# Bucketed attention and MoE on one core: exponentials interleaved in pairs of key tiles, one subtraction moved to POOL, the order made anew

## The chip, the cores and the metric

The kernel runs on one core of a Trainium2 chip. The metric is the time of one execution on the device, in microseconds (us). The program drives five engines that run side by side, each through its own queue in order: PE (TensorE, matrix products; PEld is its loading of weights), DVE (VectorE), ACT (ScalarE), POOL (GpSimd), and SP (SyncE), which here only issues transfers. Results of PE land in PSUM, eight banks of 512 fp32 columns on 128 partitions; everything else works in SBUF.

## What is computed

Two stages. Attention in which a query sees only the keys of its own bucket (six sign bits of a projection), and a feed-forward layer with squared ReLU over the result:

```python
q_bits = (np.einsum('bhsd,dk->bhsk', q, proj) > 0)          # k_bits likewise
q_bucket = np.sum(q_bits * powers, axis=-1)                 # k_bucket likewise
mask = q_bucket[:, :, :, None] == k_bucket[:, :, None, :]
scores = scale * np.matmul(q, k.transpose(0, 1, 3, 2))
scores = np.where(mask, scores, -1000000000.0)
scores = scores - np.max(scores, axis=-1, keepdims=True)
attn = np.exp(scores)
attn = attn / (np.sum(attn, axis=-1, keepdims=True) + 1e-09)
x = np.matmul(attn, v)            # then (B, H, S, D) -> (B*S, H*D)
r = np.maximum(x @ w_in, 0.0)
out = (s * (r * r) + b) @ w_out
```

There are 4 batches, 8 heads, 768 positions and 64 channels; the layer has 3072 rows, 512 inputs and 2048 hidden units. All data is fp32.

## The kernel before, in words

**Tiling.** Scores are held transposed, keys on partitions and queries along the free axis. A slot is one head and one chunk of 256 queries against all 768 keys, that is six key tiles of 128, two to a PSUM bank, so three banks of 512 columns. There are 96 slots: batch 0 first does chunk 0 of its eight heads (slots 0 to 7), then chunks 1 and 2 of each head (slots 8 to 23); batches 1 to 3 do three chunks head by head (slots 24 to 95). A visit is a run of slots with the same head.

**Two halves of a number.** [...] Where precision is needed, a number is written as a high part (fp32r) and a low part (the rest), and products run over both.

**A slot.** PE makes the scores with the mask in them (`lead`, L522). DVE takes the maximum over the six tiles for each partition and query (L527, `mx`). PE transposes that (L531), DVE takes the maximum across (L533, `nmt`), PE transposes it back (L535), DVE lays it out as rows (L541), and PE subtracts it by adding a product to the scores (`rest`, L552). ACT then takes the exponential, one bank at a time, into the three pieces of tile `et` (L557). In slots 24 to 95 each piece is then split: ACT copies the high part (L574, `hl`), POOL subtracts it for the low part (L575), and PE multiplies the values with both (L581, L582). DVE sums the exponentials over the six tiles (L603, `zb`), ACT and POOL split that (L604, L605), and PE sums it across partitions (L609). After every second head DVE takes a reciprocal (L619), POOL multiplies and splits (L620, L622), and the result goes to DRAM and comes back as the input of the MoE (`xd`, `xc`). In slots 0 to 23 the values are multiplied in plain fp32 (L579), with the sums from a column of ones, so L574, L575 and L603 do not occur.

**Before a visit.** For batches 1 to 3 queries and keys of the visit after next are transposed (L384), split (L386, L387), hashed (L409 to L411, L414) and spread by transfers; the sum of the values comes from L485. In batch 0 the first eight slots work on fp32 copies (`eq`, `ek`) and the second visits take their halves from these (`resplit`): for the queries ACT copies (L431) and POOL subtracts (L433), for the keys ACT copies (L438) and DVE subtracts (L441), each with transfers on SP's queue.

**MoE.** A unit is one batch and one chunk, 12 in all, of 8 steps each: 24 matmuls of 256 columns (L657), ReLU, square and split (L662 to L665), 12 matmuls of 512 columns (L674), and at the end L682. The weights come in pieces that are decoded in batch 0 (`decode`, L303 to L316: ACT, DVE L306 and L307, POOL L308, L315 and L316).

**The order.** Nothing is issued as it is written. Each step is added to a plan with its engine, an assumed cost, what it reads and writes, and a priority; `Plan.order` then simulates five engines and, whenever one is free, gives it the ready step with the lowest priority number. MoE steps rank behind attention, and so fill PE's gaps. The order that comes out is fixed in the program: on the chip each engine goes through its queue whether the assumed costs hold or not. The plan counts 1.75 us for L603, 1.65 for L441, and starts 1.3 decodings per slot in slots 8 and on (`RATE`), all held back further by when a buffer comes free.

The layout of the sum's input is this line, in which `es` walks, for each of 256 queries `n`, over three banks `b` and two tiles `m` that lie 256 elements apart:

```python
es = ET.rearrange("p b (m n) -> p n b m", n=CH)
dve(S * TPC, lambda: nc.vector.tensor_reduce(ZB, es, AX.XY, ALU.add), ...
```

Of the kernel before, what the change touches and what calls it, by code (L numbers as in the profile page):

```python
# [109 lines left out]
def lsh_attention_moe(ctx: ExitStack, tc, q, k, v, proj, w_in, w_out, s, b, out):  # L110
# [313 lines left out]
    def resplit(w, i, pr):  # L424

        x, h = visits[w]["x"], visits[w]["h"]
        aq, bq, ks, e = AQ[x], BQ[x], KS[x], f"e{h}"
        q_, k_ = EQ[h][:, 0:S], EK[h][:, 0:S]

        def queries(i, pr):  # L430
            act(S, lambda: nc.scalar.copy(aq[0:D], q_[0:D]), AK(e), AK(x, r=(0,)), pr)  # L431
            dma(lambda: bq[D:P], lambda: aq[0:D], AK(x, r=(0,)), BK(x, r=(1,)), pr, D * S * 4)
            pool(S, lambda: nc.gpsimd.tensor_tensor(bq[0:D], q_[0:D], f32(aq[0:D]), ALU.subtract), AK(e) + AK(x, r=(0,)), BK(x, r=(0,)), pr, 2.0)  # L433
            dma(lambda: aq[D:HR], lambda: q_[D:HR], AK(e), AK(x, r=(1,)), pr, MR * S * 4)
            dma(lambda: aq[HR:HR + TPC], lambda: bq[0:TPC], BK(x, r=(0,)), MK(x) + AK(x, r=(1,)), pr, S * 4)

        def keys(i, pr):
            act(S, lambda: nc.scalar.copy(ks[0:D, 0], k_[0:D]), KK(e), KK(x, (0,)), pr)  # L438
            dma(lambda: ks[TPC:D, 1], lambda: ks[TPC:D, 0], KK(x, (0,)), KK(x, (3,)), pr, D * S * 4)
            dma(lambda: ks[HR:HR + TPC, 0], lambda: ks[0:TPC, 0], KK(x, (0,)), KK(x, (4,)), pr, S * 4)  # L440
            dve(S, lambda: nc.vector.tensor_tensor(ks[D:P, 1], k_[0:D], f32(ks[0:D, 0]), ALU.subtract), KK(e) + KK(x, (0,)), KK(x, (1,)), pr, 1.65)  # L441
            dma(lambda: ks[D:HR, 0], lambda: k_[D:HR], KK(e), KK(x, (2,)), pr, MR * S * 4)
        return [queries, keys]
# [10 lines left out]
    def prep_values(w, pr):  # L454
# [28 lines left out]
        if not bb:  # L483
            return
        dve(NT * D, lambda: nc.vector.tensor_reduce(vp, to.rearrange("p t d -> p d t"), AX.X, ALU.add), ["vn"], ["vp"], pr, 0.6)  # L485
        pe(0.25, lambda: nc.tensor.matmul(bank[0:D, 4, CH:CH + 1], vp, ones, start=True, stop=True), ["vp"], [("b", 4, 1)], pr)
# [5 lines left out]
    def et(z):  # L492
        return E[z] if z < NE else HL[z - NE]

    def ek(z):
# [10 lines left out]
    def scores(i, pr):  # L506
# [31 lines left out]
        def rows():  # L538
            o = bank[0:TPC, 4, 0:P].rearrange("p (j n) -> p j n", j=1).broadcast_to([TPC, TPC, P])
            d = ident[0:TPC, 0:TPC].rearrange("p (j n) -> p j n", n=1).broadcast_to([TPC, TPC, P])  # L540
            nc.vector.scalar_tensor_tensor(mr.rearrange("p (j n) -> p j n", j=TPC), o, -FLOOR, d, ALU.min, ALU.mult)  # L541
        dve(CH, rows, [("b", 4, 0)], [mk], pr, 0.36)
        BANKS[i] = pb
# [12 lines left out]
        for p, z in enumerate(ES):  # L556
            act(512, lambda p=p, z=z: nc.scalar.activation(et(z), bank[:, pb[p]], AF.Exp), [("b", pb[p])], [ek(z)], pr + EP)  # L557
        PIECES[i] = ES
# [4 lines left out]
    def values(i, pr, pieces):  # L563
# [6 lines left out]
        for p in range(NP_):  # L570
            z, y = PIECES[i][p], nhl[0] % NHL
            nhl[0] += 1
            if not exact:
                act(512, lambda z=z, y=y: nc.scalar.copy(HL[2 * y], E[z]), [("e", z)], [("hl", 2 * y)], pr)  # L574
                pool(512, lambda z=z, y=y: nc.gpsimd.tensor_tensor(HL[2 * y + 1], E[z], f32(HL[2 * y]), ALU.subtract), [("e", z), ("hl", 2 * y)], [("hl", 2 * y + 1)], pr, 1.3)  # L575
            def mm(m, p=p, z=z, y=y):
# [24 lines left out]
        else:  # L601
            es = ET.rearrange("p b (m n) -> p n b m", n=CH)
            dve(S * TPC, lambda: nc.vector.tensor_reduce(ZB, es, AX.XY, ALU.add), [("e", z) for z in range(NE)], ["zb"], pr, 1.75)  # L603
# [111 lines left out]
    for i in range(NSL):  # L715
# [27 lines left out]
        if h == H - 1:  # L743
            todo.append(moe(bb, c))
        while todo and next(todo[0], True):
            todo.pop(0)
# [7 lines left out]
FIRST = 2  # L754
RATE = 1.3
SPLIT = (0, 1, 2, 3, 4, 5, 6, 7)
PACE = 2
WARM = 3
ODD = ()
FB = (5, 6, 7)  # L760
WP = -8
# [30 lines left out]
```

## Time and profile before

| | us |
|---|---|
| median of 3 runs | 1184.03 (1174.18 to 1184.86) |
| profiled execution, its own time | 1182.03 |
| its span, first to last instruction | 1180.2 |
| PE busy | 1076.2 (91%) |
| DVE busy | 760.6 (64%) |
| ACT busy | 693.2 (59%) |
| POOL busy | 668.0 (57%) |
| mean granted TensorE clock | 0.972 |

Busy times are sums over the span, and a busy PE need not be PE at its peak: matmuls overlap, and their ends are modelled. In the groups of instructions each row gives the line, the engine, the operation, what it writes and reads, the shape, the count, then the busy time and the mean of one in ns, and behind the second bar the idle time of the engine just before them with what ended it. A timeline's row gives the start, the length, the engine and the line. A row of windows gives the stretch and, for each engine, its busy time in it.

### The profile page before, as it was taken

The page shows a single profiled execution, that of the slowest core. Times are in us where ns is not written, and L with a number is a line of the kernel's source. Part 1 is how long each engine was busy: PE and PEld are TensorE (multiplying, and loading weights), DVE is VectorE, ACT ScalarE, POOL GpSimd, SP SyncE. Part 2 cuts the span into 40 slices and gives each one's busy share as a digit, 9 for nine tenths or more (in the row PEclk, how much of TensorE's full clock was granted, in tenths as well). Part 3 has the DMA queues.
Part 4 walks back from the last instruction along what each step waited for, and adds up shares of the span by engine and source line. Part 5 has one row for each costly group of instructions (what it writes and reads, how often), then busy time and mean ns, then how long its engine had stood idle before and what let it go on. Part 6 is the DMA issues. An engine that isn't in the chain of part 4 may idle for free.

```text
span 1180.2 us, 18849 instructions
## 1 busy us (share of the span) xinstructions
PE 1076.2 (91%) x6862; PEld 922.2 (78%) x6862; DVE 760.6 (64%) x815; ACT 693.2 (59%) x1377; POOL 668.0 (57%) x609
## 2 busy tenths in 40 slices
PE   8997877899899989879999998999899999999998
PEld 6665756787787778668878887888787888988987
DVE  7786783776877778777878787878787865000000
ACT  5776665656556666556766666666666666333332
POOL 4466785574656656565757575667666666222222
PEclk9998887999999999989999999999999999999999
DMA  8744443323324322332233242323223202011010
GB/s 190 197 130 125 127 120 92 109 60 84 87 63 100 90 47 74 92 82 51 71 86 95 50 113 68 78 50 104 65 67 95 66 10 82 1 54 54 1 54 18
DMA packets 99405, 94.49 MB, mean 80 GB/s; under 512 B 68529, under 2 KB 72113, under 8 KB 99313
## 3 DMA queue, kind: packets, MB, share of 16 engines
q1 hardware_dynamic: 94112, 76.24, 24.8%
q10 hardware_dynamic: 5200, 17.05, 4.9%
q8 instruction: 54, 0.88, 0.3%
q14 instruction: 39, 0.31, 0.1%
HBM read 49.81 MB, written 18.87 MB: 58 GB/s over the span
## 4 chain that ended last, share of the span: by engine, by line
PE 51%; DVE 25%; issue 11%; ACT 7%; DMA 4%; POOL 1%; SPq 1%; DVEq 0%; ACTq 0%; POOLq 0%
PE bank L657 14%; PE bank L674 12%; DVE mx L527 9%; DVE zb L603 9%; ACT et L557 5%; PE bank L552 4%; PE bank L579 3%; PE bank L531 3%; PE bank L582 2%; PE bank L581 2%; PE bank L520 2%; DMA xc<-xd 2%; PE bank L522 1%; DVE nmt L533 1%; PE bank L535 1%
## 5 line engine op out<-in xcount | busy, mean ns | idle before, releaser
L575 POOL TENSOR_TENSOR hl<-et,hl 128x512 fp32r<-128x512 f32 x216 | 272.7, 1292 | 181.2 <-ACT hl L574 169.1
L657 PE MATMUL bank<-xc,w 128*128 128x256 f32 x2304 | 350.5, 291 | 9.6 <-DMA xc<-xd 4.9
L657 PEld LDWEIGHTS bank<-xc,w 128*128 128x128 f32 x2304 | 312.0, 193 | 21.7 <-ACT rb L662 8.5
L674 PE MATMUL bank<-w,ghb 128*128 128x512 f32 x768 | 257.0, 398 | 0.0
L603 DVE TENSOR_REDUCE zb<-et 128x256 f32<-128x1536 f32 x72 | 213.7, 2968 | 36.2 <-ACT et L557 33.8
L665 POOL TENSOR_TENSOR glb<-rb,ghb 128x512 fp32r<-128x512 f32 x96 | 124.2, 1293 | 155.9 <-ACT ghb L664 142.7
L527 DVE TENSOR_REDUCE mx<-bank 128x256 f32<-128x1536 f32 x96 | 167.9, 1749 | 38.0 <-PE bank L522 24.4
L674 PE MATMUL bank<-w,glb 128*128 128x512 f32 x384 | 152.4, 399 | 0.0
L557 ACT ACTIVATE et<-bank 128x512 f32<-128x512 f32 x240 | 125.7, 597 | 41.9 <-PE bank L552 29.6
L674 PEld LDWEIGHTS bank<-w,ghb 128*128 128x128 f32 x768 | 136.7, 189 | 16.7 <-DVE osb L682 0.2
L662 ACT ACTIVATE rb<-bank 128x512 f32<-128x512 f32 x96 | 57.0, 593 | 144.3 <-PE bank L657 136.8
L581 PE MATMUL bank<-hl,vs 128*128 128x256 f32 x432 | 122.0, 301 | 1.5 <-ACT hl L574 1.1
L522 PE MATMUL bank<-aq,ks 78*128 78x256 f32 x528 | 118.3, 309 | 3.5 <-DMA xc<-xd 2.2
L574 ACT CAST hl<-et 128x512 fp32r<-128x512 f32 x216 | 119.8, 618 | 0.9
L582 PE MATMUL bank<-hl,vs 128*128 128x256 f32 x432 | 114.8, 286 | 2.7 <-POOL hl L575 2.7
L682 DVE SCALAR_TENSOR_TENSOR osb<-bank,misc,bcs 128x512 f32<-128x512 f32 x22 | 16.2, 745 | 133.8 <-PE bank L674 133.8
L522 PEld LDWEIGHTS bank<-aq,ks 78*128 78x128 f32 x528 | 90.4, 196 | 13.9 <-ACT ex L557 2.3
L613 ACT ACTIVATE xpb<-bank,vmn 64x256 f32<-64x256 f32 x96 | 44.9, 468 | 82.7 <-PE bank L582 80.1
L582 PEld LDWEIGHTS bank<-hl,vs 128*128 128x128 f32 x432 | 83.2, 192 | 6.7 <-POOL hl L575 3.9
L552 PE MATMUL bank<-bq,ks 128*128 128x256 f32 x528 | 82.8, 294 | 4.9 <-DVE bq L541 4.8
L581 PEld LDWEIGHTS bank<-hl,vs 128*128 128x128 f32 x432 | 82.8, 192 | 5.5 <-ACT hl L574 1.6
L619 DVE RECIPROCAL zpb<-zpb 128x256 f32<-128x256 f32 x48 | 83.6, 1742 | 2.2 <-ACT zpb L611 1.7
(111 smaller groups left out, 1658.0 us busy)
## 6 DMA issues: line engine op xcount, KB each, us to landing
xd<-xsb SPq DMA_DIRECT2D x48, 256.0 KB
xc<-xd SPq DMA_DIRECT2D x48, 256.0 KB
raw<-in_moe_w_in_dram ACTq DMA_DIRECT2D x16, 512.0 KB
raw<-in_moe_w_out_dram ACTq DMA_DIRECT2D x16, 512.0 KB
nat<-in_q_dram SPq DMA_DIRECT2D x32, 192.0 KB
nat<-in_k_dram SPq DMA_DIRECT2D x32, 192.0 KB
bq<-aq SPq DMA_DIRECT2D x32, 192.0 KB
out_dram<-osb SPq DMA_DIRECT2D x22, 256.0 KB
```

What stands on the lines that cost most here:

```text
L522: nc.tensor.matmul(o, ks[0:HR + TPC, 0, kt], aq[0:HR + TPC, cs], start=m == 0, stop=m == 1, skip_group_check=True)
L527: dve(S * TPC, lambda: nc.vector.tensor_reduce(t, sc, AX.XY, ALU.max), [("b", b) for b in pb], [tk], pr, 1.75)
L552: nc.tensor.matmul(o, ks[:, 1, kt], bq[:, cs], start=False, stop=m == 1, skip_group_check=True)
L557: act(512, lambda p=p, z=z: nc.scalar.activation(et(z), bank[:, pb[p]], AF.Exp), [("b", pb[p])], [ek(z)], pr + EP)
L574: act(512, lambda z=z, y=y: nc.scalar.copy(HL[2 * y], E[z]), [("e", z)], [("hl", 2 * y)], pr)
L575: pool(512, lambda z=z, y=y: nc.gpsimd.tensor_tensor(HL[2 * y + 1], E[z], f32(HL[2 * y]), ALU.subtract), [("e", z), ("hl", 2 * y)], [("hl" ...
L581: nc.tensor.matmul(av, VS[w % 2][:, kt], HL[2 * y][:, ms], start=(kt == 0), stop=False)
L582: nc.tensor.matmul(av, VS[w % 2][:, kt], HL[2 * y + 1][:, ms], start=False, stop=(kt == NT - 1))
L603: dve(S * TPC, lambda: nc.vector.tensor_reduce(ZB, es, AX.XY, ALU.add), [("e", z) for z in range(NE)], ["zb"], pr, 1.75)
L657: nc.tensor.matmul(hp, wt[("wi", n, cc)][:, m % 2, fs], xc[:, m // 2, :], start=(cc == 0 and m == 0), stop=(cc == NC_ - 1 and m == 2))
L665: pool(2 * CH, lambda r=r, gh=gh, gl=gl: nc.gpsimd.tensor_tensor(gl, r, f32(gh), ALU.subtract), [rk, hk], [lk], MP)
L674: nc.tensor.matmul(bank[:, 6 + t, :], (gh, gh, gl)[n][:, ts], wt[("wo", f)][:, n % 2], start=(f == 0 and n == 0), stop=(f == NF - 1 and n ...
```

## The change

Four things. The two key tiles of a bank are interleaved where the exponentials are written, so that the elements of a pair lie next to each other (`pairs`), and the sum, the copy and the subtraction read them so. The low part of the keys at the second visits is made on POOL instead of DVE. The planner's costs of two small operations and its `RATE` are other numbers (`GATE` is 0 and shuts nothing out). The order of all queues is made from these.

```diff
-            dve(S, lambda: nc.vector.tensor_tensor(ks[D:P, 1], k_[0:D], f32(ks[0:D, 0]), ALU.subtract), KK(e) + KK(x, (0,)), KK(x, (1,)), pr, 1.65)
+            pool(S, lambda: nc.gpsimd.tensor_tensor(ks[D:P, 1], k_[0:D], f32(ks[0:D, 0]), ALU.subtract), KK(e) + KK(x, (0,)), KK(x, (1,)), pr, 2.0)
...
-        dve(NT * D, lambda: nc.vector.tensor_reduce(vp, to.rearrange("p t d -> p d t"), AX.X, ALU.add), ["vn"], ["vp"], pr, 0.6)
+        dve(NT * D, lambda: nc.vector.tensor_reduce(vp, to.rearrange("p t d -> p d t"), AX.X, ALU.add), ["vn"], ["vp"], pr, 0.84)
...
+    def pairs(z):
+        return E[z].rearrange("p (n m) -> p m n", m=2)
...
-        dve(CH, rows, [("b", 4, 0)], [mk], pr, 0.36)
+        dve(CH, rows, [("b", 4, 0)], [mk], pr, 0.41)
...
-            act(512, lambda p=p, z=z: nc.scalar.activation(et(z), bank[:, pb[p]], AF.Exp), [("b", pb[p])], [ek(z)], pr + EP)
+            act(512, lambda p=p, z=z: nc.scalar.activation(et(z) if plain(i) else pairs(z), bank[:, pb[p]] if plain(i) else bank[:, pb[p]].rearrange("p (m n) -> p m n", n=CH), AF.Exp), [("b", pb[p])], [ek(z)], pr + EP)
...
-                act(512, lambda z=z, y=y: nc.scalar.copy(HL[2 * y], E[z]), [("e", z)], [("hl", 2 * y)], pr)
-                pool(512, lambda z=z, y=y: nc.gpsimd.tensor_tensor(HL[2 * y + 1], E[z], f32(HL[2 * y]), ALU.subtract), [("e", z), ("hl", 2 * y)], [("hl", 2 * y + 1)], pr, 1.3)
+                act(512, lambda z=z, y=y: nc.scalar.copy(HL[2 * y].rearrange("p (m n) -> p m n", n=CH), pairs(z)), [("e", z)], [("hl", 2 * y)], pr)
+                pool(512, lambda z=z, y=y: nc.gpsimd.tensor_tensor(HL[2 * y + 1].rearrange("p (m n) -> p m n", n=CH), pairs(z), f32(HL[2 * y]).rearrange("p (m n) -> p m n", n=CH), ALU.subtract), [("e", z), ("hl", 2 * y)], [("hl", 2 * y + 1)], pr, 1.3)
...
-            es = ET.rearrange("p b (m n) -> p n b m", n=CH)
+            es = ET.rearrange("p b (n m) -> p n b m", m=2)
...
-        while todo and next(todo[0], True):
+        while todo and i >= GATE and next(todo[0], True):
...
-RATE = 1.3
+RATE = 1.0
...
+GATE = 0
```

Lines from L494 on stand three lower in the changed kernel (L527 is L530 there, L603 is L606, L575 is L578). Three places show what moves. The first is in batch 0, in the slots of the second visits. DVE's queue there before:

```order
L527 TENSOR_REDUCE mx<-bank 128x256
L306 TENSOR_SCALAR raw_1100<-osb 128x512
L533 TENSOR_REDUCE nmt<-bank 128x2
L307 SCALAR_TENSOR_TENSOR osb<-osb,raw_1100 128x512
L541 SCALAR_TENSOR_TENSOR bq_71<-bank,ident 2x256
L306 TENSOR_SCALAR raw_1105<-osb 128x512
L307 SCALAR_TENSOR_TENSOR osb<-osb,raw_1105 128x512
L441 TENSOR_TENSOR ks_73<-ek_88,ks_73 64x768
L527 TENSOR_REDUCE mx<-bank 128x256
```

DVE's queue there now:

```order
L530 TENSOR_REDUCE mx<-bank 128x256
L306 TENSOR_SCALAR raw_1159<-osb 128x512
L536 TENSOR_REDUCE nmt<-bank 128x2
L307 SCALAR_TENSOR_TENSOR osb<-osb,raw_1159 128x512
L544 SCALAR_TENSOR_TENSOR bq_71<-bank,ident 2x256
L622 RECIPROCAL zpb<-zpb 128x256
L530 TENSOR_REDUCE mx<-bank 128x256
```

Between two maxima there is one decoding less, L441 is gone, and a reciprocal has come in. POOL's queue at the same place, where L441 now stands (`ek_88` is the fp32 copy of the same head's keys), behind a decoding's low part:

```order
L308 TENSOR_TENSOR osb<-osb,raw_1159 128x512
L623 TENSOR_TENSOR xpb<-xpb,zpb 128x256
L433 TENSOR_TENSOR bq_71<-eq_80,aq_69 64x768
L625 TENSOR_TENSOR xsb<-xpb,xsb 128x256
L316 TENSOR_TENSOR w_1339<-osb,w_1339 128x512
L441 TENSOR_TENSOR ks_73<-ek_88,ks_73 64x768
L623 TENSOR_TENSOR xpb<-xpb,zpb 128x256
```

POOL had L433 and the decodings at this place, and has L441 two to three rows behind each L433 now. The second place is ACT near slot 18, where the first third of the queries of batch 1 is written (L386, into `aq_68`, the buffer that the second visit of head 6 still fills by transfers). Before:

```order
L662 ACTIVATE rb<-bank 128x512
L611 ACTIVATE zpb<-bank 64x256
L613 ACTIVATE xpb<-bank,vmn 64x256
L386 ACTIVATE aq_68<-bank,misc 128x256
L663 ACTIVATE rb<-rb 128x512
L664 CAST ghb<-rb 128x512
L557 ACTIVATE et<-bank 128x512 x3
L310 CAST w_1551<-osb 128x512
```

Now:

```order
L560 ACTIVATE et<-bank 128x512 x3
L304 ACTIVATE osb<-raw_1362 128x512
L305 ACTIVATE raw_1362<-raw_1362 128x512
L431 CAST aq_69<-eq_82 64x768
L310 CAST w_1553<-osb 128x512
L614 ACTIVATE zpb<-bank 64x256
L616 ACTIVATE xpb<-bank,vmn 64x256
L438 CAST ks_73<-ek_90 64x768
L303 DMA raw_1508<-in_moe_w_out_dram 128x1024
L386 ACTIVATE aq_68<-bank,misc 128x256
```

L386 stood ahead of the three exponentials into `et` and stands behind them now, with one decoding and the copies of the next visit between. The third place is DVE in batch 2, where the sum and the maximum stand (`vp` is the sum of the values, `bq_70` the queries' buffer). Before:

```order
L615 TENSOR_TENSOR xpb<-xpb,bank 64x256
L485 TENSOR_REDUCE vp<-vn 128x64
L387 SCALAR_TENSOR_TENSOR bq_70<-bank,misc,aq_68 128x256
L603 TENSOR_REDUCE zb<-et 128x256
L527 TENSOR_REDUCE mx<-bank 128x256
L533 TENSOR_REDUCE nmt<-bank 128x2
```

Now:

```order
L618 TENSOR_TENSOR xpb<-xpb,bank 64x256
L485 TENSOR_REDUCE vp<-vn 128x64
L387 SCALAR_TENSOR_TENSOR bq_70<-bank,misc,aq_68 128x256
L606 TENSOR_REDUCE zb<-et 128x256
L530 TENSOR_REDUCE mx<-bank 128x256
L536 TENSOR_REDUCE nmt<-bank 128x2
```

Nothing moved here. From batch 2 on DVE's queue reads the same but for a few rows; in batch 1 the small steps of the preparation (L387, L414, L485) stand elsewhere in their slots, and the maximum still mostly stands right behind the sum.

## The prediction

> **What bounds the kernel now.** I read the windows first, cut where the work changes: eight first slots to 78 us, the rest of batch 0 to 250 us, the other batches to 985 us, and a tail. A slot is one head and one chunk of 256 queries.
>
> ```profile
> 0.00:78.00 78.00, 73.87 (x408) 50.45 (x409) 59.16 (x110) 53.05 (x101) 39.50 (x39) 0.96 0.71 178
> 78.00:250.00 172.00, 138.64 (x717) 113.28 (x716) 120.32 (x122) 107.60 (x206) 114.75 (x95) 0.88 0.39 110
> 250.00:985.00 735.00, 672.90 (x4530) 586.33 (x4530) 566.62 (x568) 467.32 (x964) 463.87 (x436) 0.99 0.28 73
> 985.00:1180.00 195.00, 190.82 (x1212) 172.15 (x1211) 14.52 (x16) 65.27 (x109) 49.87 (x41) 1.00 0.12 40
> ```
>
> After the length come PE, PEld, DVE, ACT and POOL busy. The tail is MoE alone and full (190.82 of 195). Batches 1 to 3 have 72 slots of 10.2 us (735/72); PE is busy 92%, no other engine over 77%. Then the chain of waits, for the price of PE work nothing holds up, and the timeline of one slot:
>
> ```profile
> 1008.88 2.88 PE bank L657 x24
> 1011.76 2.75 PE bank L674 x12
> ```
>
> ```profile
> 644.93 2.98 DVE L603 TENSOR_REDUCE zb<-et 128x256 f32<-128x1536 f32 x1 [0.41 <-ACT et L557]
> 645.60 0.40 PE L522 MATMUL bank<-aq,ks 78*128 78x256 f32 x2
> 647.83 1.75 DVE L527 TENSOR_REDUCE mx<-bank 128x256 f32<-128x1536 f32 x1
> 649.73 0.41 PE L531 MATMUL bank<-ident,mx 128*128 128x128 f32 x2 [0.34 <-DVE mx L527]
> 650.24 0.42 DVE L533 TENSOR_REDUCE nmt<-bank 128x2 f32<-128x256 f32 x1 [0.67 <-PE bank L531]
> ```
>
> One MoE step of 36 matmuls takes 5.63 us, a 256-column matmul 0.12. In the slot the sum of exponentials (L603) starts when the last exponential ends. The maximum of the next scores (L527) stands behind it on DVE, though its scores were there at 646.00: it waits 1.83 us for DVE alone. Then PE waits for the maximum, and the row of maxima leads to the next exponentials. So the loop in batches 1 to 3 runs through L603, and PE, which fills the gaps with MoE, is near its own limit. The groups between 250 and 985 us say how near:
>
> ```profile
> L603 DVE TENSOR_REDUCE zb<-et 128x256 f32<-128x1536 f32 x71 | 210.7, 2968 | 34.2 <-ACT et L557 31.8 <-POOL xsb L622 0.8 <-POOL glb L665 0.8
> L527 DVE TENSOR_REDUCE mx<-bank 128x256 f32<-128x1536 f32 x72 | 125.8, 1747 | 4.9 <-ACT zpb L611 2.7 <-PE bank L522 1.6
> L531 PE MATMUL bank<-ident,mx 128*128 128x128 f32 x144 | 31.0, 298 | 29.8 <-DVE mx L527 11.6 <-DVE bq L387 11.6 <-DVE nat L414 5.8
> L384 PE MATMUL bank<-ident,nat 128*128 128x128 f32 x138 | 28.5, 288 | 6.4 <-DVE bq L541 2.2 <-DVE nmt L533 1.4 <-ACT vmn L452 1.1
> L535 PE MATMUL bank<-ident,nmt 128*2 128x128 f32 x72 | 19.8, 275 | 6.9 <-DVE bq L387 2.2 <-ACT aq L386 1.6 <-DVE nmt L533 1.2
> L531 PEld LDWEIGHTS bank<-ident,mx 128*128 128x128 f32 x144 | 14.9, 142 | 48.7 <-DVE bq L387 14.9 <-DVE mx L527 10.7 <-ACT aq L386 8.8
> ```
>
> PE's largest idle time there, 29.8 us, lies before L531 and ends with DVE: the maximum, or L387 and L414, which stand behind it.
>
> **The change, part by part.** (a) The sum reads neighbours. Its price in the new layout is in no row. Bounds: L527, the same 1536 elements in the same number of outputs, read from PSUM, 1.75 us; L603 itself, 2.97, where every element lies 1 KB from the last. A second SBUF reduce, L485 below, reads 256 bytes apart, and its 384 elements take 836 ns: 2.2 ns an element with the start, as L603's 1.9 and unlike L527's 1.1. What is slow is thus far reads from SBUF, not the operation, so I take L527's 1.75, a cut of 1.22 us, or 72 x 1.22 = 87.8 us of DVE. [...] No run here shows pairs.
>
> How much of 87.8 comes off the path? The maximum can move up by the whole 1.22 (it waits 1.83 needlessly). PE cannot follow all the way, since most of what stands ahead of L531 is its own work. Lower end: its idle time before L531, 29.8. Upper end: 87.8, if PE's other gaps close too. Between them: a matmul of the trace counts 0.28 us or more but issues every 0.12, so each wait is understated by some 0.16, 72 x 0.16 = 11.5, giving 41.3 (the weight loads' idle time, 48.7, says nearly the same). L535 and L384 stand in the same chain two steps on, and half their idle time, (6.9 + 6.4)/2 = 6.6, should go as the row of maxima comes on time. I take 47, ends 30 and 88.
>
> (b) Exponentials are written, and copied and subtracted from, at a step of 8 bytes. The rows for that step are the weight decoding, L305 (read and write) on ACT and L308 (one operand) on POOL, beside their dense kin:
>
> ```profile
> L575 POOL TENSOR_TENSOR hl<-et,hl 128x512 fp32r<-128x512 f32 x216 | 272.7, 1292 | 181.2 <-ACT hl L574 169.1
> L557 ACT ACTIVATE et<-bank 128x512 f32<-128x512 f32 x240 | 125.7, 597 | 41.9 <-PE bank L552 29.6
> L574 ACT CAST hl<-et 128x512 fp32r<-128x512 f32 x216 | 119.8, 618 | 0.9
> L308 POOL TENSOR_TENSOR osb<-osb,raw 128x512 int32<-128x512 int32 x32 | 44.9, 1402 | 57.8 <-DVE osb L307 34.4 <-ACT xpb L613 5.7 <-ACT ex L557 4.8
> L316 POOL TENSOR_TENSOR w<-osb,w 128x512 fp32r<-128x512 f32 x32 | 42.0, 1318 | 7.6 <-ACT w L310 7.6
> L305 ACT ACTIVATE raw<-raw 128x512 int32<-128x512 uint32 x32 | 21.3, 665 | 0.0
> L485 DVE TENSOR_REDUCE vp<-vn 128x64 f32<-128x384 f32 x24 | 20.1, 836 | 0.4 <-PE bank L486 0.4
> ```
>
> On ACT 665 against 618, some 47 ns; on POOL 1402 against 1318, 84 ns. A slot has three of each: 0.14 on L557, 0.14 on L574, 0.25 on POOL. Cover:
>
> ```profile
> 625.49 3.79 POOL L575 TENSOR_TENSOR hl<-et,hl 128x512 fp32r<-128x512 f32 x3 [2.22 <-ACT hl L574]
> 630.51 0.28 PE L582 MATMUL bank<-hl,vs 128*128 128x256 f32 x1
> ```
>
> POOL's third low part ends at 629.28 and PE uses it at 630.51: 1.23 us of slack, of which (a) takes 47/72 = 0.65. The remaining 0.58 holds 0.14 + 0.25. The 0.14 on the exponentials lies on the loop, but PE's own work covers it in most slots: ends 0 and 72 x 0.14 = 10, I take +2.
>
> (c) L441, the low part of the keys, goes from DVE to POOL, eight instructions.
>
> ```profile
> L441 DVE TENSOR_TENSOR ks<-ek,ks 64x768 fp32r<-64x768 f32 x8 | 25.6, 3200 | 1.6 <-PE bank L552 1.4
> L433 POOL TENSOR_TENSOR bq<-eq,aq 64x768 fp32r<-64x768 f32 x8 | 16.1, 2018 | 11.3 <-ACT aq L431 10.2 <-DMA raw<-in_moe_w_out_dram 0.4 <-PE bank L552 0.4
> ```
>
> ```profile
> L531 PE MATMUL bank<-ident,mx 128*128 128x128 f32 x36 | 8.1, 310 | 13.7 <-DVE mx L527 12.9 <-DVE bq L387 0.3 <-DVE nat L414 0.2
> ```
>
> ```profile
> 164.43 4.91 DVE L441 TENSOR_TENSOR ks<-ek,ks 64x768 fp32r<-64x768 f32 x1
> 165.00 0.59 PE L522 MATMUL bank<-aq,ks 78*128 78x256 f32 x2
> 169.37 1.76 DVE L527 TENSOR_REDUCE mx<-bank 128x256 f32<-128x1536 f32 x1
> ```
>
> The row of L531 is that of 78 to 250 us. Here the scores were there at 165.59 and the maximum started at 169.37: L441 cost 3.78. The order has L441 right ahead of a maximum all six times in this stretch; PE's wait for maxima in it is 12.9 in all, and a plain handover of some 0.1 in each of 18 slots (36 transposes) stays. Ends 0 and 12.9; I take -11. On POOL each costs L433's 2.02, 12 us for the six in the stretch, into 172 - 114.75 = 57 us of idle time; there it waits for ACT's L438, and the decoding (L308, L316) queues behind it, for which ACT and in the end MoE wait; PE needs the keys two slots later. The DMAs of that step read ACT's high part and keep their places but for a row or two.
>
> (d) The order made anew, the weight decoding at 1.0 per slot instead of 1.3 (in the order at most two slots later), the costs of two small operations. From batch 2 on DVE's order is nearly the same; in batch 1 small steps of the preparation (L387, L414, L485) change places, for better or worse, which I cost at nothing, with the maxima's 1.83 us of spare time as cover. What matters is in batch 0:
>
> ```profile
> 188.27 0.56 SPq L145 DMA_DIRECT2D aq<-bq  x1
> 197.62 0.47 ACT L386 ACTIVATE aq<-bank,misc 128x256 fp32r<-128x256 f32 x1 [7.42 <-DMA aq<-bq]
> 198.15 0.37 PE L535 MATMUL bank<-ident,nmt 128*2 128x128 f32 x1 [7.39 <-ACT aq L386]
> ```
>
> L386 waits 7.42 us at the head of ACT's queue for a transfer, and PE with it. In the new order L386 stands one slot lower, behind three more exponentials, and the transfer is ahead of the same POOL step: the landing, 9.3 us after its issue, fits in a slot of 10. Ends 0 and -7.4 (and +7 if the new place meets another transfer); I take -6. In PE's order 64.7 instead of 64.25 MoE steps stand before the last attention matmul: 0.4 x 5.63, -2 off the tail.
>
> Sum: -47 + 2 - 11 - 6 - 2 = -64. The profiled execution took 1182.03 us (span 1180.2), 2 below the median of 1184.03: 1182 - 64 = 1118 us.
>
> **The rivals.** *Half a gain in the sum*: only the second of each pair is fast, (2.97 + 1.75)/2 = 2.36, a cut of 0.61 or 44 us of DVE, of which three quarters come through, since small cuts lie within PE's wait: -33, and with the rest 1132. For it: no row of pairs. Against: nothing either.
>
> *No gain in the sum*: the layout is not what makes it slow (something else of SBUF reads), so (a) is 0 and with (c) and (d) 1182 - 19 = 1163. Against it: L485 and L603 agree with each other and not with L527, but both read SBUF and L527 reads PSUM, so it isn't excluded.
>
> *All of it*: PE's remaining gaps close as well and 88 come through: 1182 - 88 - 19 = 1075. Against it: 92% busy.
>
> *Slower*: POOL's low part (L575) pays much more for 8-byte steps. [...] It decides from 1.23/3 = 0.41 us more per instruction on; L308 shows 0.08.
>
> **How the numbers follow.** My forecast 0.60, with its own range 1096 to 1142 (terms (a) 30 to 68, (c) and (d) failing or not); half a gain 0.12; all of it 0.08; no gain 0.12; slower 0.06; 0.02 for what I don't see. I predict 1118 us. The range 1090 to 1164 leaves out all of it, half of no gain, and slower. About 1% (12 us) is what a measurement can tell from no change. Faster by over 1%, under 1172: 0.60 + 0.12 + 0.08 + two thirds of no gain = 0.88; within 1%: 0.06; slower: 0.06.
>
> **What would show it.** L603's successor at 1.7 to 1.8 us; idle time of PE before L531's successor between 250 us and the tail fallen from 29.8 to under 10; slots of 9.5 us; the maximum in batch 0 right behind its scores; no 7 us wait of L386; ACT's exponentials under 650 ns and POOL's low parts under 1.4 us; a tail of still 190 us. Wrong would be a sum above 2.3 us, PE waiting for POOL at L582's successor, or new waits of PE for the keys in batch 0.

## The result, and the profile after

| | us |
|---|---|
| median after, 4 runs | 1119.32 (1116.31 to 1122.19) |
| median before, 4 runs of the same comparison | 1183.98 (1174.18 to 1184.86) |
| ratio, with its 95% interval | 0.9471 (0.9413 to 0.953) |
| profiled execution after, its own time | 1122.19 |
| its span | 1120.4 |

The kernel became 5.3% faster, 62.6 us by the ratio (1184 x 0.0529), where the prediction had 64. The ratios here and below leave out two slow executions, one of the kernel before at 1195 us and one of e6_step4 at 1992 us, which the medians include. To compare stages, both traces are cut at the same work: at the start of the maximum of slot 8, of slot 24 and of slot 95 (the last). The windows of the kernel before, then of the kernel after, so cut; the columns are the stretch, its length, busy time of PE, PEld, DVE, ACT and POOL, the mean granted TensorE clock, the DMA share and GB/s:

```profile
0.00:97.80 97.80, 92.02 (x481) 62.91 (x482) 71.65 (x124) 65.37 (x124) 50.15 (x48) 0.91 0.66 170
97.80:250.70 152.90, 121.19 (x649) 101.48 (x648) 107.85 (x108) 95.96 (x183) 104.80 (x87) 0.90 0.39 107
250.70:978.40 727.70, 666.18 (x4487) 580.58 (x4486) 562.05 (x563) 462.34 (x954) 457.96 (x430) 0.99 0.29 74
978.40:1180.20 201.80, 196.83 (x1250) 177.24 (x1248) 19.05 (x21) 69.58 (x117) 55.08 (x47) 1.00 0.12 39
```

```profile
0.00:106.90 106.90, 97.83 (x481) 66.70 (x482) 66.74 (x120) 64.20 (x123) 51.96 (x49) 0.87 0.58 152
106.90:244.30 137.40, 116.58 (x639) 95.72 (x638) 95.38 (x105) 95.05 (x180) 109.67 (x89) 0.94 0.45 123
244.30:920.20 675.90, 651.10 (x4508) 581.21 (x4507) 477.16 (x561) 473.21 (x957) 465.93 (x433) 0.99 0.31 79
920.20:1120.40 200.20, 195.48 (x1239) 175.46 (x1237) 17.82 (x21) 70.02 (x118) 56.38 (x48) 1.00 0.12 39
```

Line by line: slots 0 to 8 lost 9.1 us, slots 8 to 24 won 15.5, the 71 slots of batches 1 to 3 won 51.8 (10.25 to 9.52 us a slot), the tail won 1.6; together 59.8 of span. In slots 8 to 24 PE's idle time fell from 31.7 to 20.8 us, and its clock was granted at half for 15.9 us instead of 30.9 (20.9 instead of 29.3 in a second execution of both), worth 4 to 7.5 us; no term of the prediction covers the clock there. In batches 1 to 3 DVE has 85 us less to do, nearly the sum's 71 x 1.22 = 87, and PE stands idle 24.8 us (675.90 - 651.10) instead of 61.5. The groups of instructions after, in that third stretch (244.3 to 920.2 us):

```profile
L606 DVE TENSOR_REDUCE zb<-et 128x256 f32<-128x1536 f32 x71 | 124.3, 1751 | 39.4 <-ACT et L560 39.0
L530 DVE TENSOR_REDUCE mx<-bank 128x256 f32<-128x1536 f32 x71 | 124.3, 1750 | 3.4 <-ACT hl L577 1.4 <-PE bank L525 1.4
L534 PE MATMUL bank<-ident,mx 128*128 128x128 f32 x142 | 29.3, 288 | 3.2 <-DVE mx L530 1.2 <-DVE nat L414 0.7 <-DVE bq L387 0.5
L538 PE MATMUL bank<-ident,nmt 128*2 128x128 f32 x71 | 19.2, 271 | 5.0 <-ACT aq L386 4.5 <-DVE nat L414 0.4
L384 PE MATMUL bank<-ident,nat 128*128 128x128 f32 x134 | 26.9, 282 | 4.2 <-ACT zpb L614 1.5 <-DVE bq L544 1.5 <-DVE nmt L536 0.6
```

The sum (L606) takes 1751 ns, the same as the maximum (L530, 1750), which reads as many elements from PSUM. PE's wait ahead of the maximum's transpose (L534) is 3.2 us where it was 29.8. A slot of that stretch, from the timeline after (start, length, engine, line):

```profile
588.35 1.75 DVE L606 TENSOR_REDUCE zb<-et 128x256 f32<-128x1536 f32 x1 [0.54 <-ACT et L560]
588.74 0.40 PE L525 MATMUL bank<-aq,ks 78*128 78x256 f32 x2
590.02 1.75 DVE L530 TENSOR_REDUCE mx<-bank 128x256 f32<-128x1536 f32 x1
592.22 0.38 PE L534 MATMUL bank<-ident,mx 128*128 128x128 f32 x2
593.35 0.36 DVE L536 TENSOR_REDUCE nmt<-bank 128x2 f32<-128x256 f32 x1
```

The maximum still stands behind the sum, and its scores (ready at 589.14) still wait for DVE, but 0.88 us instead of 1.83; it ends at 591.77, and PE comes to the transpose at 592.22 without a wait. In this slot PE no longer waits for DVE. In batch 0 the timeline after shows a maximum that starts 0.10 us after its last scores, and L386 near slot 18 with hardly a wait:

```profile
166.03 0.59 PE L525 MATMUL bank<-aq,ks 78*128 78x256 f32 x2
166.72 1.76 DVE L530 TENSOR_REDUCE mx<-bank 128x256 f32<-128x1536 f32 x1 [0.33 <-PE bank L525]
205.74 0.47 ACT L386 ACTIVATE aq<-bank,misc 128x256 fp32r<-128x256 f32 x1 [0.24 <-PE bank L538]
```

The price of 8-byte steps, from the page's groups after (whole span):

```profile
L578 POOL TENSOR_TENSOR hl<-et,hl 128x512 fp32r<-128x512 f32 x216 | 278.1, 1317 | 163.0 <-ACT hl L577 147.6 <-PE bank L525 13.7 <-PE bank L677 1.6
L560 ACT ACTIVATE et<-bank 128x512 f32<-128x512 f32 x240 | 130.7, 624 | 31.2 <-PE bank L555 27.6 <-PE bank L553 2.7 <-POOL zhl L608 0.3
L577 ACT CAST hl<-et 128x512 fp32r<-128x512 f32 x216 | 128.6, 661 | 0.8
```

Against 1292, 597 and 618 ns before that is 25, 27 and 43 ns each. The 27 is a mean over 240 exponentials of which 24, in slots 0 to 23, are still dense, so the others cost some 30 more.

### The profile page after: what moved, and what is told of

Read it like the earlier page. It is cut to its first block, busy times and chain, and to the rows that moved or that the text cites. A ratio compares the mean times of both kernels' runs of the same rounds, so it can differ in the third digit from the quotient of the medians.

```text
span 1120.4 us, 18819 instructions
## 1 busy us (share of the span) xinstructions
PE 1061.0 (95%) x6862; PEld 919.1 (82%) x6862; DVE 657.1 (59%) x807; ACT 702.5 (63%) x1377; POOL 683.9 (61%) x617
## 4 chain that ended last, share of the span: by engine, by line
PE 80%; DVE 7%; ACT 5%; DMA 3%; POOL 3%; issue 2%; SPq 0%; DVEq 0%; ACTq 0%; POOLq 0%
PE bank L660 23%; PE bank L677 21%; PE bank L555 5%; PE bank L525 5%; PE bank L582 4%; PE bank L585 4%; PE bank L584 4%; PE bank L523 2%; PE bank L534 2%; PE bank L384 2%; PE bank L612 2%; DVE mx L530 2%; DMA xd<-xsb 2%; DMA xc<-xd 1%; ACT et L560 1%
## 5 line engine op out<-in xcount | busy, mean ns | idle before, releaser
L578 POOL TENSOR_TENSOR hl<-et,hl 128x512 fp32r<-128x512 f32 x216 | 278.1, 1317 | 163.0 <-ACT hl L577 147.6
L660 PE MATMUL bank<-xc,w 128*128 128x256 f32 x2304 | 344.8, 288 | 9.5 <-DMA xc<-xd 8.0
L660 PEld LDWEIGHTS bank<-xc,w 128*128 128x128 f32 x2304 | 307.5, 191 | 20.9 <-DMA xc<-xd 9.3
L530 DVE TENSOR_REDUCE mx<-bank 128x256 f32<-128x1536 f32 x96 | 168.1, 1752 | 44.0 <-PE bank L525 25.7
L677 PE MATMUL bank<-w,glb 128*128 128x512 f32 x384 | 152.1, 400 | 0.5 <-POOL glb L668 0.5
L560 ACT ACTIVATE et<-bank 128x512 f32<-128x512 f32 x240 | 130.7, 624 | 31.2 <-PE bank L555 27.6
L606 DVE TENSOR_REDUCE zb<-et 128x256 f32<-128x1536 f32 x72 | 126.1, 1751 | 41.3 <-ACT et L560 41.0
L577 ACT CAST hl<-et 128x512 fp32r<-128x512 f32 x216 | 128.6, 661 | 0.8
L555 PE MATMUL bank<-bq,ks 128*128 128x256 f32 x528 | 79.5, 287 | 9.6 <-DVE bq L544 8.3
```

The source lines that it names most:

```text
L530: dve(S * TPC, lambda: nc.vector.tensor_reduce(t, sc, AX.XY, ALU.max), [("b", b) for b in pb], [tk], pr, 1.75)
L555: nc.tensor.matmul(o, ks[:, 1, kt], bq[:, cs], start=False, stop=m == 1, skip_group_check=True)
L560: act(512, lambda p=p, z=z: nc.scalar.activation(et(z) if plain(i) else pairs(z), bank[:, pb[p]] if plain(i) else bank[:, pb[p]].rearrange ...
L577: act(512, lambda z=z, y=y: nc.scalar.copy(HL[2 * y].rearrange("p (m n) -> p m n", n=CH), pairs(z)), [("e", z)], [("hl", 2 * y)], pr)
L660: nc.tensor.matmul(hp, wt[("wi", n, cc)][:, m % 2, fs], xc[:, m // 2, :], start=(cc == 0 and m == 0), stop=(cc == NC_ - 1 and m == 2))
L677: nc.tensor.matmul(bank[:, 6 + t, :], (gh, gh, gl)[n][:, ts], wt[("wo", f)][:, n % 2], start=(f == 0 and n == 0), stop=(f == NF - 1 and n ...
```

## The experiments

The kernels are compared by the same four stretches (lengths in us, from one profiled execution each, cut at the starts of the maxima in its trace):

| | median | ratio to before (95%) | slots 0 to 8 | 8 to 24 | 24 to 95 | tail |
|---|---|---|---|---|---|---|
| before | 1184 | | 97.8 | 152.9 | 727.7 | 201.8 |
| after | 1119.3 | 0.9471 (0.9413 to 0.953) | 106.9 | 137.4 | 675.9 | 200.2 |
| layout alone (e1_layout) | 1131.2 | 0.9596 (0.9522 to 0.9671) | 93.7 | 149.3 | 682.7 | 202.3 |
| L441 on POOL alone (e2_keys) | 1182.5 | 1.0002 (0.9969 to 1.0034) | 100.3 | 152.1 | 730.0 | 201.9 |
| all but the layout (e3_rest) | 1167.0 | 0.988 (0.9826 to 0.9934) | 103.2 | 136.8 | 722.8 | 200.8 |
| order alone (g_order) | 1169.5 | 0.9902 (0.9872 to 0.9933) | 101.6 | 139.4 | 728.0 | 200.8 |
| after, L441 back on DVE (e7_keysback) | 1122.6 | 0.9507 (0.9445 to 0.9569) | 101.1 | 140.8 | 676.5 | 200.2 |
| after, RATE 1.3 (e5_rate) | 1125.4 | 0.9515 (0.9459 to 0.9571) | 104.1 | 141.8 | 677.3 | 200.2 |

**The layout alone.** The kernel before with the interleaved exponentials, in the order of before, row by row:

```diff
-            es = ET.rearrange("p b (m n) -> p n b m", n=CH)
+            es = ET.rearrange("p b (n m) -> p n b m", m=2)
```

(with `pairs` in the exponentials, the copy and the subtraction as in the change).

> The kernel before with the interleaved pieces alone (part a and b); every queue in the order of before. If the sum is what the time hangs on, as the prediction has it: L603's successor at 1.75 us, slots 24 to 95 some 45 us shorter, batch 0 and the tail as before, 1137 us in all (ratio 0.96). Rival, that the new order does it: 1165 us or more here, although the sum is as fast.

Measured: 1131.2 us, 48 us less than before (39 to 57). Its third stretch in the windows:

```profile
243.00:925.70 682.70, 653.20 (x4477) 581.54 (x4476) 477.60 (x563) 470.31 (x954) 460.94 (x429) 0.99 0.30 79
```

Of the 48, 45.0 are there (727.7 to 682.7). The layout gives what it was forecast to give, with every queue as it was.

**L441 on POOL alone.** The kernel before, planned as if L441 were on DVE, so that all queues keep their order, and issued to POOL:

```diff
-            dve(S, lambda: nc.vector.tensor_tensor(ks[D:P, 1], ...
+            dve(S, lambda: nc.gpsimd.tensor_tensor(ks[D:P, 1], ...
```

> The kernel before with L441 issued on POOL, at the place in the issue order where DVE had it; all other queues as before (part c alone). By the prediction the maxima of batch 0 start right behind their scores and 78 to 250 us shorten by some 11 us, 1172 us in all (ratio 0.99). Rival, that POOL's queue gets too full there and keys or decodings come late: no change or a few us more, 1182 to 1190.

Measured: 1182.5 us, ratio 1.0002 (0.9969 to 1.0034). The 11 us did not come. The groups of this kernel between 78 and 250 us:

```profile
L531 PE MATMUL bank<-ident,mx 128*128 128x128 f32 x36 | 7.8, 298 | 3.2 <-DVE bq L387 1.4 <-ACT aq L386 1.1 <-DVE mx L527 0.5
L522 PE MATMUL bank<-aq,ks 78*128 78x256 f32 x96 | 30.5, 404 | 7.4 <-ACT ex L557 7.0 <-ACT et L557 0.4
L310 ACT CAST w<-osb 128x512 fp32r<-128x512 f32 x24 | 14.9, 622 | 10.9 <-POOL osb L308 10.9
```

The row of L522 in the kernel before, in the same stretch:

```profile
L522 PE MATMUL bank<-aq,ks 78*128 78x256 f32 x99 | 29.8, 387 | 1.3 <-ACT et L557 0.6 <-ACT ex L557 0.4
```

PE's wait for maxima did go, 12.9 to 0.5 us. But PE now waits 7.0 us for exponentials into `ex` ahead of the next scores, where that was 0.4. The timeline shows how:

```profile
171.80 1.82 POOL L441 TENSOR_TENSOR ks<-ek,ks 64x768 fp32r<-64x768 f32 x1
173.69 1.26 POOL L315 TENSOR_TENSOR bcs<-bcs,osb 128x512 f32<-128x512 f32 x1
174.91 1.26 POOL L316 TENSOR_TENSOR w<-osb,w 128x512 fp32r<-128x512 f32 x1
176.13 1.29 POOL L308 TENSOR_TENSOR osb<-osb,raw 128x512 int32<-128x512 int32 x1
177.45 0.62 ACT L310 CAST w<-osb 128x512 fp32r<-128x512 f32 x1 [3.71 <-POOL osb L308]
179.93 1.55 ACT L557 ACTIVATE ex<-bank 128x512 f32<-128x512 f32 x3
180.56 0.80 PE L522 MATMUL bank<-aq,ks 78*128 78x256 f32 x2 [2.69 <-ACT ex L557]
```

L441 holds up the decodings behind it on POOL; ACT's L310 waits for the last of them at the head of its queue; the exponentials of attention stand behind L310 (with L621, L304 and L305 between); PE waits for them. Of the 12.4 us won, 6.6 went there, and the rest, as far as the rows show, into small waits on ACT (ReLU of the MoE 1.9, L386 1.1) and into PE work that took longer, with 5.7 us more at half clock in slots 8 to 24 of this execution, worth 2.8 us. Which part of that is L441's and which the execution's can't be told from one trace; that L441 on POOL by itself is worth nothing here is measured.

**L441 and the order, without the layout.** The kernel after, in its own order, with the old layout (the exponentials, the copy and the subtraction are dense again too):

```diff
-            es = ET.rearrange("p b (n m) -> p n b m", m=2)
+            es = ET.rearrange("p b (m n) -> p n b m", n=CH)
```

> The changed kernel with dense pieces and the far-reading sum again (parts c and d without a and b); every queue in the changed order. By the prediction 1182 - 19 = 1163 us (ratio 0.982), slots 24 to 95 as before. By the trace of the changed kernel, in which slots 0 to 7 took 9 us more, only some 1174. If the new order did most of it: 1135 or less.

Measured: 1167.0 us, 14 less than before (8 to 21). Added to the 48 of the layout this is 62, the whole gain: the two parts add up, within their intervals.

**The order alone.** The kernel before, L441 on DVE and the old layout, with the planner's numbers of the change:

```diff
-RATE = 1.3
+RATE = 1.0
```

(and 0.84 and 0.41 for the two small operations).

> The kernel before with only the planner's numbers changed: RATE 1.0 and the two costs, and the order of all queues made from these. L441 stays on DVE, and the exponentials are laid out as before. In its order L441 again stands right ahead of a maximum and right behind or beside L433 on POOL, and L386 stands behind the three exponentials into et. If the 14 us that the change without its layout brought come from the new order alone (the stall of L386 gone and the rest of batch 0), 1167 to 1171 us. If L441 leaving DVE is worth its predicted 11 us only together with the new order, 1178 us, since maxima still wait for L441. Rival: the new order needs both to be worth anything, 1180 us or more.

Measured: 1169.5 us, ratio 0.9902, 11.6 us less (8 to 15). So most of the 14 is the order, and L441's move, with the order planned for it, adds some 2.6 us that these intervals can't tell from nothing. In this execution half clock lasted 12.7 us in slots 8 to 24 and 37.5 us in slots 24 to 95, where the kernel before had 30.9 and 17.1, so the medians compare the two kernels and the single stages of the table don't. PE's waits in this kernel between 78 and 250 us, with L441 still on DVE and right ahead of a maximum five times of six:

```profile
L531 PE MATMUL bank<-ident,mx 128*128 128x128 f32 x38 | 8.0, 292 | 4.8 <-DVE mx L527 4.5 <-DVE bq L387 0.3
L535 PE MATMUL bank<-ident,nmt 128*2 128x128 f32 x20 | 5.4, 271 | 8.2 <-DVE nmt L533 7.6 <-ACT vmn L452 0.4
```

The wait for maxima (L531) is 4.5 us instead of 12.9, and L386's 7.4 us are gone. But the 12.9 belong to one execution: the second one of the kernel before, below, has 9.4, and the layout alone, in the order of before, 8.3. And PE's wait for `nmt` (L535), one step on, rose to 7.6 us from 3.0 (3.8 and 5.9 in the other two). Both waits together are 12.1 us, where they were 15.9, 13.2 and 14.2. So what the new order takes away is L386's stall, and 1 to 4 us of the row of maxima. In the kernel after, with L441 on POOL as well, the two waits come to 7.2 us (2.2 and 5.0); its slots 0 to 8 have some 3 us more of idle time in exchange (below).

**L441 back on DVE in the order after.** The kernel after, planned with L441 on POOL and issued to DVE, once in three rounds and once more in five, beside the kernel after itself:

```diff
-            pool(S, lambda: nc.gpsimd.tensor_tensor(ks[D:P, 1], ...
+            pool(S, lambda: nc.vector.tensor_tensor(ks[D:P, 1], ...
```

> The changed kernel with L441 back on DVE, at the place in the order that it has on POOL, and every other queue as it is. By the prediction's term (c) it delays maxima by 3 to 4 us six times in 78 to 250 us: 1119 + 11 = 1130 us. By what the move alone did in the order before (nothing, 1182.5 beside 1182.2), the gain is not in the engine: 1119, within 4 us. Rival: the move is worth something only in the new order, where the maxima are not held by anything else: 1124 to 1128.

> The changed kernel with L441 back on DVE at the place that it has on POOL, once more, with more rounds and beside the changed kernel. In the run before five of six took 0.95 us on DVE, since POOL had no instruction under way when they started, and only one 4.2 us. By that reading the engine makes no difference in this order: within 3 us of the changed kernel's median in the same comparison. Rival: the maxima still pay 0.95 us and more each, 4 us or more slower.

Measured: 1122.6 us, then 1122.25 beside 1120.31 of the kernel after; 1.9 us apart, with intervals that overlap (0.9463 to 0.9549 and 0.9457 to 0.9537). No difference between the engines can be resolved here. Why L441 is cheap on DVE here shows in its durations: of the six in slots 8 to 24 four take 0.95 us, one 1.10 and one 4.22 (in the second run three take 0.95, the others 1.10, 1.92 and 4.23). The expectation's reason, that POOL had nothing under way, holds for the four, to within 0.1 us; the 1.10 and the 4.22 started while it had. Here is the slow one between POOL's instructions, and then a fast one, from the timeline of the first of these kernels:

```profile
121.42 1.28 POOL L315 TENSOR_TENSOR bcs<-bcs,osb 128x512 f32<-128x512 f32 x1
121.74 4.22 DVE L441 TENSOR_TENSOR ks<-ek,ks 64x768 fp32r<-64x768 f32 x1
122.66 1.26 POOL L316 TENSOR_TENSOR w<-osb,w 128x512 fp32r<-128x512 f32 x1
123.89 1.26 POOL L315 TENSOR_TENSOR bcs<-bcs,osb 128x512 f32<-128x512 f32 x1
...
160.62 0.95 DVE L441 TENSOR_TENSOR ks<-ek,ks 64x768 fp32r<-64x768 f32 x1
160.64 0.42 POOL L477 MEMSET vs<- 128x384 f32 x1
```

The slow one ends at 125.96, and less the 0.95 of a fast one that is 125.01, about where POOL's last of three arithmetic instructions in a row ends (125.15): its time fits waiting for all three and 0.95 more. The fast one ran beside a MEMSET on POOL and took 0.95. The kernel before shows the same around the L441 of 164.43 to 169.34 that the prediction priced at 3.78 us:

```profile
163.81 2.27 POOL L433 TENSOR_TENSOR bq<-eq,aq 64x768 fp32r<-64x768 f32 x1
166.05 1.26 POOL L315 TENSOR_TENSOR bcs<-bcs,osb 128x512 f32<-128x512 f32 x1
167.27 1.25 POOL L316 TENSOR_TENSOR w<-osb,w 128x512 fp32r<-128x512 f32 x1
168.49 1.98 POOL L308 TENSOR_TENSOR osb<-osb,raw 128x512 int32<-128x512 int32 x1
```

Its last 0.95 us begin at about 168.4 (169.34 - 0.95), where L316 ends (168.52), and L308 beside them, 1.30 us in the median of that kernel, took 1.98. So L441 took 0.95 us beside a MEMSET and 4.22 and 4.91 beside arithmetic; why both take longer side by side is not shown. How many of POOL's instructions L441's time covers differs. Twice above it is three, although they follow one another; once in the first of these kernels it was only the rest of one, and POOL's next instruction, 0.74 us in the median, took 1.45:

```profile
146.95 1.28 POOL L316 TENSOR_TENSOR w<-osb,w 128x512 fp32r<-128x512 f32 x1 [1.25 <-ACT w L310]
147.94 1.10 DVE L441 TENSOR_TENSOR ks<-ek,ks 64x768 fp32r<-64x768 f32 x1
148.18 1.45 POOL L623 TENSOR_TENSOR xpb<-xpb,zpb 128x256 f32<-128x256 f32 x1
```

What decides between the two is not shown. So of L441's price 0.95 us was the instruction's own, and the rest was where beside POOL's queue it fell. The median of the six is 2.2 us with the order alone changed, where it was 4.0 and 3.2 in two executions of the kernel before; but it is 2.0 with the layout alone, in the order of before, so these medians don't show that the new order keeps L441 clear of POOL's work.

**RATE alone, from the other end.** The kernel after with RATE back at 1.3 and its order made from that:

```diff
-RATE = 1.0
+RATE = 1.3
```

> The changed kernel with the planner's RATE back at 1.3 and the order of all queues made from that; layout, L441 on POOL and the two costs stay. In its order L386 stands ahead of the three exponentials into et again, as before the change, and MoE starts later in batch 0 (3.6 steps at slot 24 instead of 5.4, 13.7 instead of 14.7 at slot 36, the same from slot 60 on). The prediction's term (d): the stall of 7.4 us comes back and MoE's place in the tail does not change, so 1119 + 6 = 1125 us, up to 1127. Rival: RATE is worth nothing by itself, since the order of batch 0 is bound elsewhere: within 3 us of 1119. Rival: the changed RATE is what cost the 9 us in slots 0 to 8: these then take 98 us instead of 107 and the time is below 1116.

Measured: 1125.4 us; 0.9515 (0.9459 to 0.9571) beside the 0.9471 and 0.9497 of the kernel after, so 2 to 5 us, not resolved. The trace does show L386's wait again:

```profile
198.38 0.47 ACT L386 ACTIVATE aq<-bank,misc 128x256 fp32r<-128x256 f32 x1 [6.65 <-issue]
```

PE then waits 4.31 us for the exponentials that stand behind it, and slots 8 to 24 take 141.8 us instead of 137.4 (139.0 in a second execution of the kernel after). That RATE caused the loss in slots 0 to 8 falls: they take 104.1.

**Dense exponentials, the price of 8-byte steps.** The kernel after with the writes, the copy and the subtraction dense again, while the sum still walks neighbours:

```diff
-                act(512, lambda z=z, y=y: nc.scalar.copy(HL[2 * y].rearrange("p (m n) -> p m n", n=CH), pairs(z)), ...
+                act(512, lambda z=z, y=y: nc.scalar.copy(HL[2 * y], E[z]), ...
```

> The changed kernel, but exponentials, copies and low parts are written and read densely; only the sum still reads neighbours, so it adds up other elements than those of its query. It prices the 8-byte steps of ACT and POOL (part b). By the prediction, which has +2 us for them, 1117 us, at most 10 us under the changed kernel. Rival, that the steps eat much of the gain: 1105 or less. The sum itself should take the same 1.75 us.

Measured: 1116.0 us, ratio 0.9449 (0.9396 to 0.9502). That is 3 us less than the kernel after by the medians, with intervals that overlap. Slots 24 to 95, where the steps are, took 674.1 us, against 675.9 and 676.2 in two executions of the kernel after, so the steps cost about 2 us; the forecast had 2.

**How near is near?** The tiles interleaved in runs of two queries (`c=2`, a pair is 8 bytes apart) and in runs of four (`c=4`, 16 bytes apart); the walk of the sum is the same:

```diff
-            es = ET.rearrange("p b (n m) -> p n b m", m=2)
+            es = ET.rearrange("p b (a m c) -> p a c b m", m=2, c=2)
```

> The changed kernel with the two tiles interleaved in runs of two queries instead of one: the two elements that the sum adds are 8 bytes apart, in the same 16 bytes, and the sum walks banks, then the pair, then queries as before. If what counts is that both elements lie in the same 16 bytes, the sum keeps 1.75 us and the time is 1116 to 1120 (writes in runs of 8 bytes cost no more than single ones). Rival: only direct neighbours are fast; the sum takes 2.97 us and the time is that of the run with the change but without the layout, 1167. Rival: the instruction's form with one more axis costs by itself, 2.0 to 2.4 us and 1125 to 1140.

> The changed kernel with the two tiles interleaved in runs of four queries: the two elements that the sum adds are 16 bytes apart, never in the same 16 bytes. [...] Rival: what pays is distance itself, and 16 bytes are near; the sum keeps 1.75 to 2.0 us and the time is 1116 to 1128.

Measured: 1118.8 us (ratio 0.9468, 0.9417 to 0.9519) and 1168.0 us (0.9876, 0.981 to 0.9941). The sum in the groups of the first, and then of the second:

```profile
L606 DVE TENSOR_REDUCE zb<-et 128x256 f32<-128x1536 f32 x72 | 126.1, 1751 | 41.0 <-ACT et L560 40.7
```

```profile
L606 DVE TENSOR_REDUCE zb<-et 128x256 f32<-128x1536 f32 x72 | 213.4, 2964 | 34.8 <-ACT et L560 33.5
```

At 8 bytes all of the gain is there, at 16 none: 16 bytes apart is as slow as 1 KB (2964 and 2968 ns). So direct neighbours aren't needed, and 1 KB costs no more than 16 bytes. Whether it is the distance that counts, or that a pair lies in the same 16 bytes, as all pairs 8 bytes apart do here, these runs don't decide, and no run has a distance between 8 and 16. Half a gain does not show either: every second read goes to another piece of `et`, and costs nothing that the 1751 ns, beside 1750 from PSUM, would show.

**The same two kernels again.** The kernel after and the kernel before, unaltered, profiled once more, because slots 0 to 8 had lost 9.1 us for no reason that the prediction knew.

> The changed kernel itself, unaltered, profiled and timed once more. In its first profile slots 0 to 8 took 106.9 us, with the TensorE clock at half for 28.5 us of them; other kernels with the same order there took 101 to 104 us with 16 to 23 us at half. If the clock's loss is chance from one execution to the next, these slots take 100 to 105 us this time and the half clock lasts 16 to 25 us. Rival: it belongs to this kernel, 106 to 108 us and 27 us or more. Its time is 1117 to 1122 us either way.

> The kernel before, unaltered, profiled once more. Slots 0 to 8 took 97.8 us in its first profile and 94 to 100 us in the two kernels that keep its order there, with 17 us at half clock or less. If its order by itself spares the clock there, 94 to 100 us again; if it is chance, up to 104. L441 is expected to take 3.7 us or more again wherever it starts while POOL has an instruction under way, 0.95 us otherwise, and the stall of L386 to stay at 6 to 8 us. Its time is 1180 to 1184 us.

Measured: 1120.31 and 1180.04 us. The first stretch of the second execution of the kernel after, in its windows:

```profile
0.00:99.80 99.80, 90.92 (x481) 62.08 (x482) 66.42 (x120) 64.21 (x123) 52.30 (x49) 0.93 0.62 163
```

The same work took 99.8 us instead of 106.9, at a mean granted clock of 0.93 instead of 0.87. The loss to the clock is 99.8 x 0.07 = 7.0 us in one and 106.9 x 0.13 = 13.9 in the other, and the difference, 6.9, is the 7.1 between them. So about 5 of the 9.1 us (13.9 less the 97.8 x 0.09 = 8.8 of before) are this execution's chance. Others show it too: the kernel with dense exponentials took 106.9 us there, with 28.5 us at half clock, which the expectation leaves out, and the one with L441 back on DVE 101.1 us in one run and 105.9 in the other. The rest is idle time of PE: 9.1 and 8.9 us in the two executions of the kernel after, 5.8 and 6.5 in those of the kernel before. It is 8.7 to 9.4 in every kernel that was planned with L441 on POOL, and 6.1 in the one with the new order but L441 planned on DVE, so those 3 us belong to the move's order. Before again: slots 0 to 8 took 99.6 us, and L386 waited 7.54. L441 took 0.95 to 5.1 us; two that started while POOL was at work took 2.32 and 1.91, where at least 3.7 was expected.

## Why the prediction came out right, and which of its terms did not

- **(a) The sum at 1.75 us and 47 us of it on the path: right, in mechanism and size.** That pairs run at the maximum's rate was the author's estimate, which no run before the result showed; the sum after shows it. 1751 ns; 45 us in slots 24 to 95 with the layout alone, 48 (39 to 57) in all. Of 87 us that DVE was spared half came through; PE, busy 651.1 of 675.9 us there, leaves little room for the rest. With all of the change PE's idle time in slots 24 to 95 fell by 36.7 us: 26.6 of them before L531, and 4.1 before L535 and L384, where 6.6 was expected. Its busy time fell by 15.1; some 3.5 of that is the clock (17.1 us at half in this stretch before, 10.2 after). The other 11.6 is as much as the "understated" waits were put at, but no row shows that it is these.
- **(b) +2 for 8-byte steps: right.** About 2 in slots 24 to 95. The bounds from L305 and L308 (47 and 84 ns) were high: 27, 43 and 25 ns. L308's 1402 ns was a mean that holds the 1.98 us beside L441 shown above and others like it; the median is 1295, and L316's 1270.
- **(c) -11 for L441 on POOL: wrong.** Alone it gave 0 (-4 to +4), and in the new order 2 to 3 us that the intervals don't resolve. Two steps failed. The step that read L441's 3.78 us as the price of the instruction on DVE: its own time is 0.95, and the rest came with what POOL did beside it (0.95 to 5.1 us in the same kernel). And the step that named POOL's 57 us of idle time as cover: the decodings behind L441 are waited for by ACT at the head of its queue, with attention's exponentials behind. The prediction named that chain, "for which ACT and in the end MoE wait", and costed it at nothing. Besides, the 12.9 us of waiting from which the -11 came was one execution's; the second had 9.4.
- **(d) -6 for the order, -2 off the tail: right in what it named, somewhat small.** L386's wait is gone and the tail is 1.6 shorter. The order alone is worth 11.6 (8 to 15) where 8 was forecast; beside L386's 7.4 the waits of the row of maxima fell by 1 to 4 us. Whether a share of it goes through the clock, which was at half for less time in slots 8 to 24, stays open. (c) and (d) together brought -14 (-21 to -8) where -19 was forecast.
- **What nothing in the prediction covered:** 9.1 us in slots 0 to 8, some 5 of them the clock in that execution and about 3 the order that was planned with L441 on POOL.
- **The rivals.** Half a gain would have shown a sum of 2.36 us, no gain one of 2.97: it is 1.75. All of it needed 36 us more in batches 1 to 3 (88 - 52), where PE has only 24.8 us of idle time left. The slower case needed 0.41 us more per low part on POOL: it is 0.025.

The sum came to 1118 and the time to 1119.3 because the largest term was right and the errors of the others were of both signs: (c) 8 to 11 too much, (d) about 4 too little, (a) and (b) together 3 too little (48 where 45 was forecast). That these cancel to about 1 us is luck.

## What to carry to other kernels

A reduction on DVE that reads SBUF in far steps is worth a run with its inputs laid so that two reads in a row lie close together: here it took 2968 ns with 1 KB between them, 2964 with 16 bytes, and 1751 with 8 or 4 bytes. The strided writes cost little here, 25 to 43 ns per 512 elements. Before an instruction is moved off DVE for being slow, look at its fastest instance and at what POOL does beside the others: it may be the neighbour and not the instruction (L441 took 0.95 us where it started with POOL idle or at a MEMSET, up to 5.1 beside POOL's arithmetic). And a wait that a move ends is not yet time won: ask who stands behind the moved instruction in its new queue, down to the engine that bounds. Here PE's wait for maxima went from 12.9 to 0.5 us, and the time did not change.

## What the runs showed of the hardware

The TensorE clock was granted at half in stretches of 3.41, 6.83 and 10.24 us in slots 0 to 95 of the kernels before and after (3.41, 10.24, 10.24 and the first 4.6 of 6.83 in slots 0 to 8 of the kernel after, with PE busy through all of them). Three windows in a row of the kernel after, in which half clock lasted from 44.3 to 54.5 us:

```profile
24.00:36.00 12.00, 12.00 (x50) 7.44 (x49) 8.86 (x13) 7.15 (x15) 5.02 (x4) 0.87 0.74 196
36.00:48.00 12.00, 11.50 (x58) 8.26 (x58) 7.61 (x11) 8.24 (x17) 4.08 (x4) 0.84 0.67 169
48.00:60.00 12.00, 12.00 (x54) 7.73 (x53) 7.17 (x10) 6.77 (x14) 6.24 (x6) 0.73 0.41 109
```

No long idle time of PE stands ahead of these 10 us: PE was busy all but 0.5 of the 36 (busy time as recorded, which says nothing of how full the array was). What sets the clock to half is not shown. From one execution to another of the same kernel the time at half clock in slots 0 to 8 was 28.5 and 13.3 us (16.9 and 18.5 for the kernel before), so that a comparison of one trace with one trace has 5 us or more of chance in that stage, while slots 24 to 95 repeat within 0.3 us (675.9 and 676.2, and 727.7 and 727.8 before).
